# Two attention layers with products inserted between the steps: shorter insertions at fixed steps, values returned sooner

## The chip, the cores and the metric

One core of one Trainium2 chip. The time is device microseconds (us) of one execution of the whole kernel. Matrix products run on TensorE (PE), elementwise work on VectorE (DVE), exponentials and copies on ScalarE (ACT), some small work and DMA issues on GpSimd (POOL), further DMA issues on SyncE (SP). Matmuls write to PSUM, from which ACT and DVE read; everything else lies in SBUF or, between stages, in device memory.

## What is computed

Two layers, each an attention block and a Fourier mixing block, on a sequence of 2048 rows of 640 numbers, with 32 heads of 20:

```python
def _A_ref(x, wqkv, wo):
    qkv = (x @ wqkv).reshape(B, S, 3, H, Dh).transpose(2, 0, 3, 1, 4)
    q, k, v = qkv[0], qkv[1], qkv[2]
    scores = jnp.einsum("bhqd,bhkd->bhqk", q, k) * (Dh ** -0.5)
    p = _softmax(scores, axis=-1)
    o = jnp.einsum("bhqk,bhkd->bhqd", p, v)
    return o.transpose(0, 2, 1, 3).reshape(B, S, D) @ wo
def _B_ref(x, dft_seq_re, dft_seq_im, dft_hid_re, dft_hid_im):
    a = jnp.einsum("bsd,ed->bse", x, dft_hid_re)
    b = jnp.einsum("bsd,ed->bse", x, dft_hid_im)
    return jnp.einsum("ts,bse->bte", dft_seq_re, a) - jnp.einsum("ts,bse->bte", dft_seq_im, b)
x = A_x
x = x + _A_ref(_layernorm(x), A_wqkv, A_wo)
x = x + _B_ref(_layernorm(x), ...)
x = x + _A_ref(_layernorm(x), A_wqkv, A_wo)
x = x + _B_ref(_layernorm(x), ...)
```

## The kernel before

**Steps.** The attention of a layer is 512 steps, in `Attention.sweep`. A step n is a group g of four heads (eight groups), a query block qb of 512 queries (four) and a key chunk kc of 128 keys (sixteen), kc running fastest, so kc is n mod 16. `scores(n, j)`, called for j = 0 and 1, does two matmuls (L517, two heads) into one of three PSUM tiles `p`, and one exponential on ACT (L520) from there into one of seven `e` tiles. `values(n)` does the four heads' products of `e` and v (L528, eight matmul records) into the PSUM tile `acc`, of which there is one; after kc = 15 `finish` transposes it on DVE (L535), divides by the sums and stores the block (L549). Values run behind the scores: `owed = n - 1 - done` is 1 when the values of step n - 2 are due at step n.

**What is inserted.** The attention of a layer starts when one chunk of 128 columns of q and one of k are made. The rest is a generator, `Qkv.work`, that yields blocks: four chunks of q and k, the second half of v, four more chunks. For a chunk and a block of 512 tokens (tb) a product is fifteen matmuls of 128x512 (L99) into the single PSUM tile `fill`, cut by `pieces`; behind the last piece `keep` splits the product on DVE (L84, L87, and the squares at L201) and stores it (L207), and the block yields a function `after`, which makes the norms (a matmul L212 that reads the squares, a maximum on DVE at L213) and, at the end of a chunk, splits the weights of the next. The last block computes a bound on the scores, with one tiny matmul in its `after`. When the generator ends, `done()` queues the loads of the next stage's weights as tasks.

**The order by hand.** Every step of `sweep` calls `fill(n)`, which runs a waiting `after` when its step has come, or else the next block if `rest` has passed and the line `due` allows it. Before step `THIN` = 236, 80 blocks are laid down (600 matmuls); from there 16 blocks (two chunks, pieces of eight and seven) follow a straight line to step 414. If `fill` ran a block at a step from THIN on, and fewer than three values are owed, the values of that step are held back, and at a step not before `calm` two sets are done at once, unless the set to be done ends a query block. `need` forces blocks when the coming group's q and k are not made; the last chunk of q is wanted by steps 368 (tb 0), 389, 405 and 421 (tb 3).

**DVE besides.** `compare` runs up to two checks of the Fourier matrices per step on DVE (L763, L767) with loads from POOL.

Of the kernel before, what the change touches and what calls it, by code (L numbers as in the profile page):

```python
# [19 lines left out]
ND = D // 128  # L20
NT = S // 128
# [14 lines left out]
def mha_fnet_kernel(ctx, tc, x_in, wqk, wv, wo, seq, hid, nat_seq, nat_hid, out):  # L36
# [65 lines left out]
    def pieces(blocks, n):  # L102

        todo = [f for b in blocks for f in b]
        for i in range(0, len(todo), n):
            for f in todo[i:i + n]:
                f()
            yield i + n < len(todo)
# [23 lines left out]
    class Qkv:  # L132
        def __init__(s, L, src):
            s.L, s.src = L, src
            s.xn, s.xt, s.rs, s.v = {}, {}, {}, {}
            s.scr = {qk: dr.tile([D, 2, S], F32, name=f"scr{qk}_{L}") for qk in "qk"}
            s.shift = {n: dr.tile([H, 2, c], F32, name=f"shift{n}_{L}") for n, c in (("b", 512), ("m", S))}
            s.n = 1
            s.made, s.raw = set(), {}


        def load(s, k):
# [238 lines left out]
        def work(s):  # L381

            order = [ND + 1, 1, ND + 2, 2, ND + 3, 3, ND + 4, 4]
            w = {0: s.w1}

            def chunk(i):
                c = order[i]
                for tb in range(NB):
                    p = bank("fill", [128, 512], "pqk")
                    for more in pieces([s.product(p, w[i], tb, dc) for dc in range(ND)], 8):  # L390
                        if more:
                            yield True
                    sq = s.keep(p, c, tb, True, s.fill)

                    def after():
                        s.norms(bank("fill", [H, 512], "pn"), c, tb, sq)
                        s.made.add((c, tb))
                        if tb == NB - 1:
                            s.made.add(c)
                            if i + 1 < len(order):  # L400
                                w[i + 1] = s.weights(s.fill("w", [2, ND, 128], F32R, "wqk"), order[i + 1], True)
                            if i + 2 < len(order):
                                s.fetch(order[i + 2])
                    yield after

            for i in range(4):
                yield from chunk(i)
            for t in range(NT):
                p = bank("fill", [128, HD], "pv")
                for more in pieces([s.value(p, t, dc) for dc in range(ND)], 8):  # L410
                    if more:
                        yield True
                s.own(p, t, 1, True)
                yield None
            s.made.add("v")
            for i in range(4, 8):
                yield from chunk(i)

            r = s.bounds()
            ok = const.tile([128, 1], F32, name="ok", bufs=2)  # L420
            V.tensor_scalar(ok[:H], r[:H, 2:3], (GUARD / SCALE) ** 2, None, op0=OP.is_le)

            def after():
                p = bank("fill", [1, 1], "pok")
                PE.matmul(p, ok[:H], one[:H], start=True, stop=True)
                V.tensor_scalar(s.flag, p, float(H), None, op0=OP.is_equal)
            yield after
# [25 lines left out]
    class Attention:  # L453
# [98 lines left out]
        def sweep(s, shift, begin, fill):  # L552
            done = calm = 0
            for n, (g, qb, kc) in enumerate(s.steps):
                begin(n, g, qb, kc)
                last = qb == NB - 1
                if kc == (7 if last else 10 if g == LATE else 4) and not (last and g == H // 4 - 1):
                    s.qload(*((g, qb + 1) if not last else (g + 1, 0)), shift)
                if last and g + 1 < H // 4:
                    for f, j in {1: [(0, 0)], 9: [(0, 1)], 11: [(1, 0)]}.get(kc, []):  # L560
                        s.kload(g + 1, f, j)
                if qb == 0 and kc == 0 and g:
                    s.kload(g, 1, 1)
                s.scores(n, 0)
                s.scores(n, 1)

                more, owed = fill(n) and n >= 2 and n + 1 < len(s.steps), n - 1 - done
                if n < s.THIN:  # L570
                    if more and kc != 1:
                        continue
                    count = owed
                else:
                    if more and owed < 3:
                        calm = n + 6
                        continue
                    count = min(owed, 1)
                    if owed > 1 and (done + 1) % NT and n >= calm:
                        calm = n + 6  # L580
                        count = 2
                for _ in range(count):
                    s.values(done)
                    done += 1
            for n in range(done, len(s.steps)):
                s.values(n)

        def run(s, done, project, check):

            work, tasks, later = s.a.work(), s.a.vweights(1, s.a.fill, pause=[lambda: None] * 2), list(check)  # L590
            s.work, s.blocks, s.after, s.rest, s.more, s.landed = True, 0, None, 0, False, 0

            marks = ((0, 0), (44, 16), (s.THIN, 80), (414, 96), (512, 130))

            def due(n):
                for (n0, k0), (n1, k1) in zip(marks, marks[1:]):
                    if n < n1:
                        return k0 + (k1 - k0) * (n - n0) / (n1 - n0)

            def block(n):  # L600
                try:
                    f = next(work)
                    s.blocks += 1
                    s.more = f is True
                    s.after = (n + 2, f) if f and not s.more else None
                    s.rest = n + 4 if s.after else n
                except StopIteration:
                    s.work = False
                    tasks.extend(done())

            def fill(n):
                if s.after:
                    if n >= s.after[0]:
                        f, s.after = s.after[1], None
                        f()
                elif s.work and n >= s.rest and (s.more and n < s.THIN or s.blocks < due(n + 1)):
                    block(n)
                    s.rest = max(s.rest, n + 2)
                    return s.work

            def compare(n):


                if n < 8:
                    return
                for _ in range(2):
                    if not later or n < s.landed or (len(check) - len(later)) * 490 >= n * len(check):
                        break
                    task = later.pop(0)
                    if isinstance(task, tuple):  # L630
                        s.landed = n + 5
                        task = task[1]
                    task()

            def need(n, *keys):
                while not all(k in s.a.made for k in keys):
                    if s.after:
                        fill(s.after[0])
                    else:
                        block(n)  # L640

            def begin(n, g, qb, kc):


                if qb == NB - 1 and g + 1 < H // 4:
                    when, to = 0, g + 1
                    c0, c1 = to * 80 // 128, ((to + 1) * 80 - 1) // 128
                    keys = [c0, (c1, 0) if to == LATE else c1, ND + c0, ND + c1] + (["v"] if to >= 4 else [])
                else:
                    when, to, keys = 5, g, [(ND - 1, qb + 1)]  # L650
                if to != g or g == LATE and qb < NB - 1:
                    if kc == when:
                        need(n, *keys)
                        s.shift = s.a.bound(to, s.room)
                    if kc - when in (0, 3, 5):
                        next(s.shift)

                if tasks and n % 2 == 0 and n >= 16 and n % 64 < 54:
                    tasks.pop(0)()
                for f in project.early.get(n, []):  # L660
                    f()

            def between(n):
                more = fill(n)
                compare(n)
                return more

            s.sweep("b", begin, between)
            assert not s.work and not later and not tasks, (len(later), len(tasks))
# [857 lines left out]
```

## Time and profile before

| | us |
|---|---|
| median of 3 runs | 2545.14 (2545.03 to 2545.29) |
| span of the profiled execution, first to last instruction | 2543.2 |
| the median less the span (launch and end; the profiled execution has no other time recorded) | 1.9 |
| PE busy, matmuls | 2507.9 |
| ACT busy | 2136.9 |
| ACT busy in exponentials (L520) | 1938.1 |
| PE busy in values (L528), scores (L517) | 1061.5, 815.1 |
| DVE busy | 977.0 |
| POOL busy | 520.3 |

How the views are read: the page groups instructions by line, engine and tiles, with busy time and the idle time before them; a row of the timeline is start, duration, engine, line, operation, output and inputs, number of instructions merged, and in brackets the idle time before it with what released it; a row of stretches is the stretch, its length, then for each engine the busy time and the number of instructions, then the granted clock, the share of the DMA engines and GB/s. PE stands for matmuls and PEld for weight loads, which overlap them. A wait is put down to the engine and line that released it.

### The profile page before, as it was taken

The page shows a single profiled execution, that of the slowest core. Times are in us where ns is not written, and L with a number is a line of the kernel's source. Part 1 is how long each engine was busy: PE and PEld are TensorE (multiplying, and loading weights), DVE is VectorE, ACT ScalarE, POOL GpSimd, SP SyncE. Part 2 cuts the span into 40 slices and gives each one's busy share as a digit, 9 for nine tenths or more (in the row PEclk, how much of TensorE's full clock was granted, in tenths as well). Part 3 has the DMA queues.
Part 4 walks back from the last instruction along what each step waited for, and adds up shares of the span by engine and source line. Part 5 has one row for each costly group of instructions (what it writes and reads, how often), then busy time and mean ns, then how long its engine had stood idle before and what let it go on. Part 6 is the DMA issues. An engine that isn't in the chain of part 4 may idle for free. (4 is left out here: it accounts for less than half of the span.)

```text
span 2543.2 us, 43630 instructions
## 1 busy us (share of the span) xinstructions
PE 2507.9 (99%) x16350; PEld 1153.8 (45%) x16350; DVE 977.0 (38%) x2114; ACT 2136.9 (84%) x2430; POOL 520.3 (20%) x1022
## 2 busy tenths in 40 slices
PE   8999999999999999999999999999999999999998
PEld 7544444443333332239885444444433333322596
DVE  6245422244333233426763343223332323232275
ACT  6688899988999999985457888999899999999752
POOL 2012111112111121113321121111111111131133
PEclk9999999999999999999999999999999999999999
DMA  5224221222322233327553332212221212133365
GB/s 186 97 85 129 87 80 45 86 89 87 95 76 84 76 95 109 117 81 244 192 180 105 110 114 82 84 52 75 85 84 48 82 50 79 51 92 101 104 220 192
DMA packets 127024, 262.52 MB, mean 103 GB/s; under 512 B 28736, under 2 KB 53088, under 8 KB 126804
## 3 DMA queue, kind: packets, MB, share of 16 engines
q1 hardware_dynamic: 88212, 159.79, 19.2%
q0 software_dynamic: 38592, 99.85, 12.5%
q8 instruction: 132, 2.16, 0.4%
q14 instruction: 88, 0.72, 0.1%
HBM read 175.29 MB, written 84.21 MB: 102 GB/s over the span
## 5 line engine op out<-in xcount | busy, mean ns | idle before, releaser
L520 ACT ACTIVATE e<-psc 128x1024 f32<-128x1024 f32 x2048 | 1938.1, 1115 | 156.3 <-PE psc L517 119.7
L528 PE MATMUL acc<-e,v 128*32 128x512 f32 x8192 | 1061.5, 602 | 3.8 <-DVE of L535 3.3
L517 PE MATMUL psc<-stq,stk 62*128 62x512 f32 x4096 | 815.1, 463 | 3.0 <-ACT e L520 3.0
L517 PEld LDWEIGHTS psc<-stq,stk 62*128 62x128 f32 x4096 | 341.3, 184 | 835.4 <-ACT e L520 787.3
L528 PEld LDWEIGHTS acc<-e,v 128*32 128x32 f32 x8192 | 187.5, 108 | 365.8 <-issue 338.3
L549 POOL DMA_DIRECT2D o<-oh x256 | 131.9, 523 | 1002.0 <-DVE oh L544 1000.7
L99 PE MATMUL pqk<-xt,wqk 128*128 128x512 f32 x1200 | 313.8, 405 | 3.7 <-DVE wqk L84 1.5
L99 PEld LDWEIGHTS pqk<-xt,wqk 128*128 128x128 f32 x1200 | 214.7, 188 | 89.2 <-issue 37.4
L535 DVE STREAM_TRANSPOSE of<-acc 128x512 f32<-128x512 f32 x64 | 45.9, 717 | 543.0 <-PE acc L528 543.0
L84 DVE CAST hl<-pqk 128x512 fp32r<-128x512 f32 x64 | 44.2, 691 | 455.2 <-PE pqk L99 455.2
L99 PE MATMUL pv<-wv,xt 128*128 128x320 f32 x960 | 159.8, 317 | 0.0
L99 PEld LDWEIGHTS pv<-wv,xt 128*128 128x128 f32 x960 | 141.1, 188 | 25.5 <-issue 21.5
L549 POOL DMA_DIRECT2D o<-ot x256 | 128.6, 510 | 1.3 <-issue 0.4
L207 POOL DMA_DIRECT2D scrq<-hl x40 | 28.2, 706 | 388.4 <-DVE hl L87 264.2
L763 DVE TENSOR_REDUCE far<-cq 128x1 f32<-128x512 f32 (+5 forms) x169 | 98.5, 584 | 5.7
L92 PE MATMUL py<-wo,o 128*128 128x320 f32 x320 | 99.2, 310 | 1.4 <-DVE xr L945 1.4
L94 PE MATMUL py<-wo,o 128*128 128x320 f32 x320 | 98.6, 308 | 0.0
L93 PE MATMUL py<-wo,o 128*128 128x320 f32 x320 | 98.6, 308 | 0.0
L767 DVE TENSOR_TENSOR cq<-cq 128x512 f32<-128x512 f32 (+4 forms) x166 | 96.4, 580 | 2.7 <-DMA cq<-in_nat_seq_dram 2.7
L243 DVE COPY v<-pv 128x320 f32<-128x320 f32 x32 | 15.7, 491 | 204.1 <-PE pv L99 204.1
L207 POOL DMA_DIRECT2D scrk<-hl x40 | 27.9, 698 | 298.3 <-DVE hl L87 248.7
L213 DVE TENSOR_REDUCE top<-pn 32x1 f32<-32x512 f32 x80 | 53.4, 675 | 31.3 <-PE pn L212 31.3
(200 smaller groups left out, 1720.7 us busy)
## 6 DMA issues: line engine op xcount, KB each, us to landing
cq<-in_nat_seq_dram POOLq DMA_DIRECT2D x64, 512.0 KB, 5.4
scrq<-hl POOLq DMA_DIRECT2D x40, 512.0 KB, 3.2
scrk<-hl POOLq DMA_DIRECT2D x40, 512.0 KB, 3.5
stq<-scrq SPq DMA_DIRECT2D x256, 80.0 KB
stk<-scrk SPq DMA_DIRECT2D x128, 160.0 KB
o<-o SPq DMA_DIRECT2D x16, 1280.0 KB
stq<-scrq SPq DMA_DIRECT2D x256, 40.0 KB
stk<-scrk SPq DMA_DIRECT2D x128, 80.0 KB
```

What stands on the lines that cost most here:

```text
L92: PE.matmul(out_ap, ah, bh, start=start, stop=False)
L93: PE.matmul(out_ap, ah, bl, start=False, stop=False)
L94: PE.matmul(out_ap, al, bh, start=False, stop=stop)
L99: yield lambda i=i, j=j, k=k: PE.matmul(out_ap, a[i], b[j], start=dc == 0 and k == 0, stop=dc == ND - 1 and k == 2)
L207: G.dma_start(s.scr["qk"[k]][c * 128:(c + 1) * 128, :, tb * 512:(tb + 1) * 512], hl.bitcast(F32))
L213: V.tensor_reduce(s.top[:H, c // ND, c % ND, tb:tb + 1], p, op=OP.max, axis=AX.X)
L517: PE.matmul(p[:, i], s.k[g, kc // 8, j][r, kc % 8 * 128:(kc % 8 + 1) * 128], s.q[g, qb, j][r], start=True, stop=True)
L520: A.activation(e, p, AF.Exp, scale=SCALE)
L528: PE.matmul(s.acc[32 * j:32 * j + 32], s.a.v[kc][:, v0:v0 + 32], s.e[n, j // 2][:, j % 2], start=kc == 0, stop=kc == NT - 1, skip_group_ch ...
L549: G.dma_start(s.o[k, h * DH:(h + 1) * DH, qb * 512:(qb + 1) * 512], hl[k][32 * j:32 * j + DH])
L763: V.tensor_reduce(to, x, op=OP.max, axis=AX.X, apply_absolute_value=True)
L767: V.tensor_tensor(y, x, y, op=op)
```

## The change

From step 236 on, the products of q and k are inserted in pieces of five matmuls, three per product and 24 in all, at fixed steps: n mod 16 in 2, 7, 12 before step 271, and 2, 10 from there, instead of on a straight line (`rest` still applies). The norms come four steps after the last piece instead of two, and the next block not before two steps after the norms. Values held back return from n + 2 on instead of n + 6. When the generator has reached its last block (`silent`), values are no longer held back for it; it and the end of the generator follow as soon as `rest` allows.

```diff
@@ class Qkv
-            s.made, s.raw = set(), {}
+            s.made, s.raw, s.silent = set(), {}, False
@@ def work
-                    for more in pieces([s.product(p, w[i], tb, dc) for dc in range(ND)], 8):
+                    for more in pieces([s.product(p, w[i], tb, dc) for dc in range(ND)], 8 if i < 6 else 5):
...
             for i in range(4, 8):
                 yield from chunk(i)
 
+            s.silent = True
             r = s.bounds()
@@ def sweep
                     if more and owed < 3:
-                        calm = n + 6
+                        calm = n + 2
                         continue
                     count = min(owed, 1)
                     if owed > 1 and (done + 1) % NT and n >= calm:
-                        calm = n + 6
+                        calm = n + 2
                         count = 2
@@ def run
-            marks = ((0, 0), (44, 16), (s.THIN, 80), (414, 96), (512, 130))
+            marks = ((0, 0), (44, 16), (s.THIN, 80))
 
             def due(n):
                 for (n0, k0), (n1, k1) in zip(marks, marks[1:]):
                     if n < n1:
-                        return k0 + (k1 - k0) * (n - n0) / (n1 - n0)
+                        return s.blocks < k0 + (k1 - k0) * (n - n0) / (n1 - n0)
+                return s.blocks < 80 or s.blocks >= 104 or (n - 1) % NT in ((2, 7, 12) if n < 272 else (2, 10))
 
             def block(n):
...
-                    s.after = (n + 2, f) if f and not s.more else None
-                    s.rest = n + 4 if s.after else n
+                    s.after = (n + (2 if n < s.THIN else 4), f) if f and not s.more else None
+                    s.rest = s.after[0] + 2 if s.after else n
...
-                elif s.work and n >= s.rest and (s.more and n < s.THIN or s.blocks < due(n + 1)):
+                elif s.work and n >= s.rest and (s.more and n < s.THIN or due(n + 1)):
                     block(n)
                     s.rest = max(s.rest, n + 2)
-                    return s.work
+                    return s.work and not s.a.silent
```

## The prediction

> **What bounds the kernel now.** I read the page first, for the size of the parts.
>
> ```profile
> span 2543.2 us, 43630 instructions
> ...
> PE 2507.9 (99%) x16350; PEld 1153.8 (45%) x16350; DVE 977.0 (38%) x2114; ACT 2136.9 (84%) x2430; POOL 520.3 (20%) x1022
> ...
> PEclk9999999999999999999999999999999999999999
> ...
> L520 ACT ACTIVATE e<-psc 128x1024 f32<-128x1024 f32 x2048 | 1938.1, 1115 | 156.3 <-PE psc L517 119.7
> L528 PE MATMUL acc<-e,v 128*32 128x512 f32 x8192 | 1061.5, 602 | 3.8 <-DVE of L535 3.3
> L517 PE MATMUL psc<-stq,stk 62*128 62x512 f32 x4096 | 815.1, 463 | 3.0 <-ACT e L520 3.0
> ```
>
> PE looks full, but the exponentials of L520 are two per step of attention, 1024 per layer, and that line is busy for three quarters of the span. To see which of the two ends last, I looked at L520 alone in stretches. The first row below holds 472 exponentials, so 609.15 is the first of step 236 in layer 0; 1870.51 is the same place in layer 1. The next stretch of each layer is 376 exponentials, steps 236 to 423 (the count of 377 takes in one that straddles the edge), and the last is 176, steps 424 to 511.
>
> ```profile
> 87.16:609.15 521.99, 456.88 (x472) 1.00 0.28 87
> 609.15:972.56 363.41, 350.70 (x377) 1.00 0.27 83
> 972.56:1133.90 161.34, 161.34 (x177) 1.00 0.33 102
> 1347.42:1870.51 523.09, 456.81 (x472) 1.00 0.27 86
> 1870.51:2233.30 362.79, 350.66 (x377) 1.00 0.23 65
> 2233.30:2394.80 161.50, 161.50 (x177) 1.00 0.29 85
> ```
>
> In steps 424 to 511 nothing is inserted and ACT is busy all the time: 161.34 / 176 = 0.917 us for each exponential, 1.834 for a step. At that pace the 376 of the middle stretch would need 344.7 us. They took 363.4 and 362.8. So inserted work costs 18.7 us in layer 0 and 18.1 us in layer 1, and these 36.8 us are all that this change can reach: steps before 236 keep their pieces of eight and their waiting rules. For the middle stretch of layer 0 the view of L520's waits gives:
>
> ```profile
>   PE psc L517: 8.2, 30
>   PE acc L528: 4.0, 17
> ```
>
> ACT idles 12.2 us there, in 47 pieces. The rest is restart: exponentials overlap in a train and do not behind a gap. A train of 13 takes 12.04 us, so (12.04 - 1.02) / 12 = 0.918 each, against 1.03 for one alone; each of the 47 gaps costs 0.11 more, 5.2 us. 12.2 + 5.2 = 17.4 of the 18.7.
>
> ```profile
> 612.92 12.04 ACT L520 ACTIVATE e<-psc 128x1024 f32<-128x1024 f32 x13 [0.20 <-PE acc L528]
> ```
>
> **The price of one piece before.** The timeline of steps 258 and 259, a piece of eight with its step's values left out, then a step with one set of values:
>
> ```profile
> 650.62 0.91 PE L517 MATMUL psc<-stq,stk 62*128 62x512 f32 x4
> 651.02 0.19 PEld L517 LDWEIGHTS psc<-stq,stk 62*128 62x128 f32 x2 [0.22 <-ACT e L520]
> ...
> 651.45 2.10 PE L99 MATMUL pqk<-xt,wqk 128*128 128x512 f32 x8
> 653.49 0.30 PEld L517 LDWEIGHTS psc<-stq,stk 62*128 62x128 f32 x4 [0.35 <-issue]
> 653.49 0.73 PE L517 MATMUL psc<-stq,stk 62*128 62x512 f32 x4
> 654.09 1.03 ACT L520 ACTIVATE e<-psc 128x1024 f32<-128x1024 f32 x1 [0.37 <-PE psc L517]
> 654.15 1.06 PE L528 MATMUL acc<-e,v 128*32 128x512 f32 x8
> 655.14 0.30 PEld L517 LDWEIGHTS psc<-stq,stk 62*128 62x128 f32 x4 [0.84 <-ACT e L520]
> 655.14 0.73 PE L517 MATMUL psc<-stq,stk 62*128 62x512 f32 x4
> 655.31 1.03 ACT L520 ACTIVATE e<-psc 128x1024 f32<-128x1024 f32 x1 [0.20 <-PE acc L528]
> ```
>
> Scores hold PE for 0.66 (653.49 to 654.15) and one set of values for 0.99, so a plain step needs 1.65 of PE and 1.83 of ACT: PE gains 0.18 of lead per step until it has to wait for a score buffer, as at 651.02. The piece of eight holds PE 2.04. Behind it ACT waits twice: 0.37 for scores, and 0.20 for the values that free the next of seven e buffers. With two restarts the piece costs 0.37 + 0.20 + 0.22 = 0.79. The rows below hold the two other parts. A piece of seven holds PE 674.57 - 672.76 = 1.81, so one matmul is 0.23, and its price is 0.79 - 0.23 = 0.56. Some steps after a piece the withheld values come back, two sets in one step (663.30), 1.85 of PE, and ACT waits 0.25, with the restart 0.36:
>
> ```profile
> 663.30 1.92 PE L528 MATMUL acc<-e,v 128*32 128x512 f32 x16
> ...
> 665.15 0.73 PE L517 MATMUL psc<-stq,stk 62*128 62x512 f32 x4
> 665.75 1.02 ACT L520 ACTIVATE e<-psc 128x1024 f32<-128x1024 f32 x1 [0.25 <-PE psc L517]
> ...
> 672.76 1.88 PE L99 MATMUL pqk<-xt,wqk 128*128 128x512 f32 x7
> 674.57 0.30 PEld L517 LDWEIGHTS psc<-stq,stk 62*128 62x128 f32 x4 [0.35 <-issue]
> ```
>
> There are eight products per layer left at step 236 (two chunks by four token blocks), each 15 matmuls, so 8 x (0.79 + 0.56 + 2 x 0.36) = 16.6. To that comes one norms product that waits for DVE's squares, at step 404:
>
> ```profile
> 931.21 0.73 PE L517 MATMUL psc<-stq,stk 62*128 62x512 f32 x4
> ...
> 933.83 0.68 DVE L201 TENSOR_TENSOR sq<-hl 128x512 bf16<-128x512 f32 x1
> ...
> 934.56 0.38 PE L212 MATMUL pn<-sq,ind 128*32 128x512 bf16 x1 [0.96 <-DVE sq L201]
> ...
> 935.91 1.94 ACT L520 ACTIVATE e<-psc 128x1024 f32<-128x1024 f32 x2 [0.94 <-PE acc L528]
> ...
> 967.12 23.94 ACT L520 ACTIVATE e<-psc 128x1024 f32<-128x1024 f32 x26 [0.17 <-PE psc L517]
> ```
>
> That is 0.94 + 0.11 = 1.05. The last row is the values withheld at step 414 for a block that inserts no matmul of size, returned at 420: 0.17 + 0.11 = 0.28. Sum 16.6 + 1.05 + 0.28 = 17.9 against 18.1 and 18.7 found. The prices account for the stretch.
>
> **The change part by part.** *Pieces of five instead of eight and seven.* Each product becomes three pieces, 24 per layer instead of 16. The second exponential behind a piece is tied to PE: it starts 655.31 - 653.49 = 1.82 after the scores that follow the piece, so its delay falls by what the piece is shorter: 0.79 - 3 x 0.23 = 0.10 for five. PE then holds 1.35 in place of 0.99.
>
> By the Trainium skill (TensorE: Matmul & The Clock Gate, section Back-to-back issue gap) a 512-column matmul takes 518 cycles, 0.216 us, behind another; three fewer would then save 0.65 and not 0.69, the price would be 0.14, and the estimate of the total 2 us higher. The rows above have 0.23, and I keep that.
>
> *Values back at n + 2 instead of n + 6.* This is the disputed part: PE has had no time to rebuild its lead. Call T the start of the scores in step n + 1. The second exponential of that step starts at T + 1.82, and in a train the first of step n + 3 would start three later, at T + 1.82 + 3 x 0.918 = T + 4.57. PE starts step n + 2 at T + 1.65, spends 0.66 + 1.85 on scores and two sets of values, starts step n + 3 at T + 4.16, and 0.60 after that (653.49 to 654.09) the exponential can start: T + 4.76. It is late by 0.19. So the early return is not dearer than the old one; ACT was already held up 0.10 by the piece and PE works at 1.65 meanwhile. Bounds: 0.19 by this walk, 0.36 by the row of the old returns. I take 0.25, nearer to the walk, because it uses PE times from rows of just such steps.
>
> *The next piece.* From step 274 pieces stand 8 apart (step mod 16 is 2 or 10), from 236 to 268 five, six or eleven. A slot at 252 is in the list but not usable: the third piece at 247 puts its norms at 251 and rest at 253. So the pieces stand at 236, 242, 247, 258, 263, 268, 274, 282 and so on to 410: 24. PE's work over 8 steps with one piece is 8 x 0.66 + 6 x 0.99 + 1.85 + 1.35 = 14.4, ACT's 14.7. It just fits. At a distance of five: from the scores of step n + 3 at U (exponential at U + 0.60) PE reaches the scores behind the next piece at U + 2 x 1.65 + 0.66 + 1.35 = U + 5.31, and the tied exponential at U + 7.13, against U + 0.60 + 7 x 0.918 = U + 7.03. Again 0.10.
>
> *Norms product at n + 4.* The squares at 404 were ready at 934.51, 3.30 after the piece's end (931.21). In the new order PE reaches the norms product after 1.65 + 2.51 + 1.65 + 0.66 = 6.5. The 1.05 goes. If it returned at the three third pieces that stand right behind the block's end (290, 338, 386), 3.2 would be added.
>
> *Silent end.* No values are withheld for the bounds block any more: 0.28 goes. The loads for the next stage start four steps later, at 422 instead of 418. I cost that at nothing: ninety steps of attention still cover them. If that cover were gone it would be those four steps, 4 x 1.83 = 7.3 in each layer. DMA issues keep their number: eight stores of hl, the same o and weight loads, on the same queues.
>
> Sum per layer: 24 x (0.10 + 0.25) = 8.4, with ends 24 x (0.10 + 0.19) = 7.0 and 24 x (0.10 + 0.36) + 3.2 = 14.2. Layer 0's surplus of 0.6 over layer 1 stays. Saved: 18.1 - 8.4 = 9.7 per layer, 19.4 in two; the ends are 22 and 8. The profiled span is 2543.2, 1.9 below the median of 2545.1, which adds what lies around it and does not change. 2545.1 - 19.4 = 2525.7, so 2526, between 2523 and 2537.
>
> **The rivals.** *PE is the real bound*, as its 99% say. Then only PE's work counts: three fives hold it 4.05 against 2.04 + 1.81, +0.20 per product, less 0.13 for one more doubled return (2 x 0.99 - 1.85): 16 x 0.07 = +1.1, 2546. Against it: 1.65 per step against 1.83, and PE waiting on ACT at 651.02.
>
> *The early return meets PE with no lead at all.* Then three steps cost what PE needs, 2.01 + 1.65 + 2.51 = 6.17 against 5.50: 0.67 x 24 = 16.1 per layer, 2.0 saved each, 2541. For it: the order of events above leaves no spare step. Against: the walk.
>
> *Slower: the norms product waits for DVE every time.* PE runs in order, so scores queue behind it and ACT behind them. The block's end puts a chain on DVE, and the checks put pairs there:
>
> ```profile
> 622.00 0.72 DVE L535 STREAM_TRANSPOSE of<-acc 128x512 f32<-128x512 f32 x1 [9.40 <-PE acc L528]
> ...
> 625.19 0.69 DVE L545 TENSOR_TENSOR ot<-ot,oh 128x512 f32<-128x512 f32 x1
> ...
> 626.07 0.67 DVE L767 TENSOR_TENSOR cq<-cq 128x512 f32<-128x512 f32 x1
> ...
> 626.78 0.69 DVE L763 TENSOR_REDUCE far<-cq 128x1 f32<-128x512 f32 x1
> ```
>
> A further chain (3.88) and a pair (1.36) ahead of the squares make 3.3 + 5.2 = 8.5, 2.0 later than PE arrives; with a restart 2.1 x 8 = 16.8 per layer, 25.2 with the 8.4, 7.1 more than now: 2559. It decides from a cost of 9.7 / 8 = 1.2 at every product. Against: DVE is 38% busy, and of the eight norms products of layer 0 one waited, at half the distance:
>
> ```profile
>   DVE sq L201: 1.0, 1
> ```
>
> *Returns cost nothing*: 24 x 0.10 = 2.4, 15.7 saved per layer, 2514. The walk speaks against it.
>
> *The slots don't hold*: if one more slot were lost the last norms would fall at 422, behind the demand of step 421, and PE would wait about 1 us in each layer: 2528.
>
> **How the numbers follow.** Forecast 0.78, slots 0.04, free returns 0.05: together 0.87 faster by over 0.2% (5 us, about what a measurement of this kernel can tell from no change). PE bound 0.03 and no lead 0.04 are within it: 0.07. Slower: 0.06, the DVE wait and what I have not seen. The range runs from 2519, where half of the returns is hidden, to 2539, a little beyond the dear end of the sum; it leaves out the rivals at 2514, 2541, 2546 and 2559 and a little of the forecast's own tails, 0.2 in all.
>
> **What would show it.** In the timeline from step 236: ACT trains broken by two short gaps per piece, about 0 to 0.1 us at the next step (released by L528's acc) and 0.1 to 0.25 at the step behind the doubled values (released by psc), no longer 0.37 and more; no L212 with an idle time released by DVE; the stretch of 376 exponentials at 353 us per layer; the stretches before step 236 unchanged at 522 and 523. It is wrong if gaps of 0.3 and more stand behind the returns, if PE waits for DVE at the norms, or if the last stretch grows by what the middle one lost.

## The result

2524.36 us (2523.62 to 2524.84) against 2545.22 for the kernel before, 20.9 less: a ratio of 0.9918, interval 0.9904 to 0.9932. The forecast was 2526, 19.4 less.

The stretches of the exponentials' line, which is L521 now since the change adds a line above it (values are L529), show where it went. Columns: the stretch, its length, ACT busy in that line and the number, granted clock, DMA share, GB/s. The first three are steps 0 to 235, 236 to 423 and 424 to 511 of layer 0, the others the same of layer 1 up to 423.

```profile
span 2522.9 us, 43616 instructions
...
87.57:609.52 521.95, 456.85 (x472) 1.00 0.28 87
609.52:961.81 352.29, 349.44 (x378) 1.00 0.28 86
961.81:1122.10 160.29, 160.29 (x177) 1.00 0.34 102
1337.49:1860.62 523.13, 456.82 (x473) 1.00 0.27 86
1860.62:2212.90 352.28, 349.43 (x377) 1.00 0.23 68
```

The first and last stretches are what they were: 521.99 and 523.09 before for the first; the 160.29 and the 161.34 of before are cut at different points inside the last exponential, and from end to end the 176 take 161.33 in both kernels. The middle fell from 363.41 to 352.29 and from 362.79 to 352.28: 11.1 + 10.5 = 21.6. The span fell by 20.3, so 1.3 went elsewhere: 0.4 ahead of the first exponential (87.58 against 87.17), 0.6 between the layers (214.0 against 213.4 from the last exponential's end to the next one's start), and 0.3 lies in where the stretches are cut. Of the 18.7 and 18.1 us that inserted work cost per layer, 7.6 are left (352.3 - 344.7). The stretches run from start to start; from the end of one exponential to the end of another it is 352.5, which is nearer to the 7.75 that the expectations below use.

What L521 waited for in the middle stretch of layer 0 (us, times):

```profile
  PE acc L529: 0.2, 1
```

And the norms product L212 in the same stretch:

```profile
  issue: 2.9, 8
```

Before, these were 8.2 and 4.0 us of idle ACT in 47 places, and one norms product waited 1.0 for DVE. Now one idle place of 0.2 is listed, and no wait for DVE. But 7.6 us are lost all the same. An exponential that comes 0.1 or 0.2 late still begins before or shortly after the last one ends, so it loses its overlap with it and leaves little idle time. The stretch has 2.85 of ACT's idle time (352.29 less 349.44), in pieces too short for the list; the other 4.7 is lost overlap, which counts as busy. Neither number alone shows the loss; the length of the stretch does. The timeline of one period, steps 258 to 261:

```profile
650.73 1.43 PE L99 MATMUL pqk<-xt,wqk 128*128 128x512 f32 x5
652.08 0.73 PE L518 MATMUL psc<-stq,stk 62*128 62x512 f32 x4
...
653.74 0.73 PE L518 MATMUL psc<-stq,stk 62*128 62x512 f32 x4
...
654.40 1.92 PE L529 MATMUL acc<-e,v 128*32 128x512 f32 x16
...
656.26 0.73 PE L518 MATMUL psc<-stq,stk 62*128 62x512 f32 x4
```

Five matmuls hold PE for 1.35 (650.73 to 652.08), as worked out from the pieces of eight and seven. With T = 652.08 the next scores start at T + 1.66 and the scores behind the doubled values at T + 4.18; the walk had T + 1.65 and T + 4.16. ACT over the same time is one unbroken row:

```profile
647.26 19.02 ACT L521 ACTIVATE e<-psc 128x1024 f32<-128x1024 f32 x20
```

In a train 20 exponentials would take 19 x 0.917 + 1.03 = 18.45. Of the 0.57 more, 0.47 are three delays around the pieces of 258 and 263 (0.10, 0.21 and 0.16 by the ends of the exponentials), without a gap that would split the row. Over the stretch it is 7.6 / 24 = 0.32 per piece. Measured from the end of each exponential to the end of the next, it is 0.10 to 0.16 at the second one behind a piece and 0.20 to 0.24 behind the doubled values, and next to nothing elsewhere; only the very first piece costs 0.30, at step 237.

### The profile page after: what moved, and what is told of

The parts are those of the page before. It is cut to its first block, busy times and chain, and to the rows that moved or that the text cites. A ratio compares the mean times of both kernels' runs of the same rounds, so it can differ in the third digit from the quotient of the medians.

```text
span 2522.9 us, 43616 instructions
## 1 busy us (share of the span) xinstructions
PE 2492.9 (99%) x16350; PEld 1152.7 (46%) x16350; DVE 976.4 (39%) x2114; ACT 2134.2 (85%) x2430; POOL 520.5 (21%) x1022
## 5 line engine op out<-in xcount | busy, mean ns | idle before, releaser
L521 ACT ACTIVATE e<-psc 128x1024 f32<-128x1024 f32 x2048 | 1935.9, 1128 | 137.1 <-PE psc L518 103.7
L529 PE MATMUL acc<-e,v 128*32 128x512 f32 x8192 | 1058.6, 602 | 1.9 <-DVE of L536 1.8
L518 PE MATMUL psc<-stq,stk 62*128 62x512 f32 x4096 | 799.3, 458 | 1.3 <-ACT e L521 1.3
L529 PEld LDWEIGHTS acc<-e,v 128*32 128x32 f32 x8192 | 188.9, 108 | 370.0 <-issue 344.7
L84 DVE CAST hl<-pqk 128x512 fp32r<-128x512 f32 x64 | 44.2, 690 | 432.2 <-PE pqk L99 432.2
L99 PEld LDWEIGHTS pv<-wv,xt 128*128 128x128 f32 x960 | 141.2, 188 | 25.5 <-issue 21.6
```

The costliest lines, as they stand in the source:

```text
L99: yield lambda i=i, j=j, k=k: PE.matmul(out_ap, a[i], b[j], start=dc == 0 and k == 0, stop=dc == ND - 1 and k == 2)
L518: PE.matmul(p[:, i], s.k[g, kc // 8, j][r, kc % 8 * 128:(kc % 8 + 1) * 128], s.q[g, qb, j][r], start=True, stop=True)
L521: A.activation(e, p, AF.Exp, scale=SCALE)
L529: PE.matmul(s.acc[32 * j:32 * j + 32], s.a.v[kc][:, v0:v0 + 32], s.e[n, j // 2][:, j % 2], start=kc == 0, stop=kc == NT - 1, skip_group_ch ...
```

## The experiments

The theory: ACT bounds these steps; what is lost is what PE's order makes an exponential late, 0.10 behind a piece of five (tied to PE through the values that free its e buffer) and 0.20 behind the return at n + 2 (PE's excess of a double step, less the lead it then has). The rivals: the early return alone is the gain; the fixed steps alone are; PE's total work is the bound. In the following the stretch is always that of the 376 exponentials of steps 236 to 423, layer 0 then layer 1, and the loss its length less 344.7.

**One part at a time.** The kernel before with the early return alone, the same edit in both places (`e1_return`):

```diff
-                        calm = n + 6
+                        calm = n + 2
```

> The kernel before with one edit: values return from n + 2 instead of n + 6; pieces of eight and seven on the straight line stay. Theory (ACT is held up by what PE does between two scores, and only a short piece shortens that): a return at n + 2 costs about 0.2 behind a piece of eight, but behind a piece of seven it falls on the step of the norms product and costs about 0.4, against 0.30 to 0.38 before; under 1 us per layer saved, 2543 to 2545, stretch of 376 exponentials 362 to 363.5. Rival (the early return is the gain): most of the 21 us is here, 2531 or less.

2546.64 us, ratio to the kernel before 1.0006 (0.9997 to 1.0015): no gain. The stretches:

```profile
609.00:971.78 362.78, 350.30 (x377) 1.00 0.27 84
1869.76:2232.20 362.44, 350.36 (x378) 1.00 0.22 66
```

0.6 and 0.4 shorter than before, as the theory has it, and too little to be seen in the time. The time itself was forecast at 2543 to 2545 and came out 1.6 above: in the profiled execution 2.3 more lie behind the last exponential of layer 1 (150.7 against 148.4), a stage that the edit does not touch; why was not tried. The early return is not the gain by itself.

The changed kernel with pieces of eight and seven again, at its fixed steps (`e3_eight`):

```diff
-    ... pieces([s.product(p, w[i], tb, dc) for dc in range(ND)], 8 if i < 6 else 5):
+    ... pieces([s.product(p, w[i], tb, dc) for dc in range(ND)], 8):
-                return s.blocks < 80 or s.blocks >= 104 or ...
+                return s.blocks < 80 or s.blocks >= 96 or ...
```

> The changed kernel with pieces of eight and seven again (16 instead of 24), at the same fixed steps, values back at n + 2. Theory: a piece costs 0.79 or 0.56 and a return 0.2 to 0.4, about 14.4 lost per layer instead of 7.75, 2538. Rival (the fixed steps are the gain): 2526 or less, since fewer pieces are inserted.

2538.84 (ratio 0.9974, 0.9964 to 0.9984).

```profile
609.04:967.67 358.63, 349.25 (x378) 1.00 0.31 92
1867.47:2226.53 359.06, 349.66 (x378) 1.00 0.26 74
```

Losses 13.9 and 14.4, forecast 14.4. Fixed steps, later norms, early return and silent end together give 6.6 us; cutting the products into fives gives the other 14.5 (2538.84 to 2524.36). By the ends of the exponentials a piece of eight costs about 0.79 and one of seven about 0.56 here, and the return behind either 0.20 to 0.23, as behind fives.

**When the values return.** `calm` set to n + 1, n + 3 or n + 4 in both places of the changed kernel (`e8_next`, `e9_three`, `e2_late`):

```diff
-                        calm = n + 2
+                        calm = n + 1    # e8_next; n + 3 in e9_three, n + 4 in e2_late
```

> The changed kernel with values back from n + 1. Theory: with two sets in step n + 1 PE starts the scores of n + 2 at T + 2.51, their exponential at T + 3.11 instead of T + 1.82 + 0.92 = T + 2.74: 0.37 late instead of 0.2, about 11.8 lost per layer instead of 7.75, 2532.5. Rival (the sooner the better): 2524 or less.

> The changed kernel with values back from n + 3. Theory: by then PE has caught up with ACT and waits for a score buffer ahead of the double step, 0.3 late instead of 0.2, about 10.5 lost per layer, 2530; n + 2 is the cheapest of n + 1 to n + 4. Rival (later is better, PE has more lead): under 2524.

> The changed kernel with one edit: values return from n + 4 (n + 6 cannot be had with pieces five steps apart). Theory: two steps later PE waits for score buffers again, the return costs 0.3 and more as in the old order, and the lead is not back at the next piece; about 12.5 lost per layer instead of 7.75, 2534. Rival (the pieces are all of the gain, the return is free): 2524 to 2526.

The stretches of e8_next:

```profile
609.08:965.55 356.47, 349.39 (x378) 1.00 0.28 84
1864.15:2220.37 356.22, 349.40 (x378) 1.00 0.23 67
```

Of e9_three:

```profile
609.23:964.59 355.36, 349.70 (x378) 1.00 0.27 85
1862.84:2218.22 355.38, 349.79 (x377) 1.00 0.23 67
```

And of e2_late:

```profile
609.05:966.94 357.89, 350.73 (x377) 1.00 0.27 84
1864.98:2222.89 357.91, 350.71 (x378) 1.00 0.23 67
```

| values back from | time, us | ratio to before (interval) | loss per layer |
|---|---|---|---|
| n + 1 | 2532.05 | 0.9949 (0.9936 to 0.9963) | 11.8, 11.5 |
| n + 2 | 2524.36 | 0.9918 (0.9904 to 0.9932) | 7.6, 7.6 |
| n + 3 | 2529.58 | 0.9938 (0.9925 to 0.9952) | 10.7, 10.7 |
| n + 4 | 2534.79 | 0.9960 (0.9946 to 0.9974) | 13.2, 13.2 |

All three were forecast within 1 us. Neither sooner nor later is better. The timeline of e8_next, steps 259 and 260, has an idle time that n + 2 avoids:

```profile
652.39 0.73 PE L518 MATMUL psc<-stq,stk 62*128 62x512 f32 x4
...
654.91 0.73 PE L518 MATMUL psc<-stq,stk 62*128 62x512 f32 x4
655.51 4.69 ACT L521 ACTIVATE e<-psc 128x1024 f32<-128x1024 f32 x5 [0.27 <-PE psc L518]
```

Scores at T + 2.52, exponential at T + 3.12 with 0.27 of idle time and 0.11 of restart, 0.38: the 0.37 of the walk. With eights and sevens the return hardly matters (`e1_return`), with fives there are 10.4 us between n + 2 and n + 4, and at n + 4 the fives save only 10.6. The two edits belong together.

**How short.** Pieces of 4, 4, 4 and 3, 32 per layer, five to six steps apart (`e7_four`):

```diff
-    ... 8 if i < 6 else 5):
+    ... 8 if i < 6 else 4):
-    ... s.blocks >= 104 or (n - 1) % NT in ((2, 7, 12) if n < 272 else (2, 10))
+    ... s.blocks >= 112 or (n - 1) % NT in (2, 7, 12)
-    s.rest = s.after[0] + 2 if s.after else n
+    s.rest = s.after[0] + (2 if n < s.THIN else 1) if s.after else n
```

> The changed kernel with pieces of 4, 4, 4 and 3 instead of three fives, 32 per layer, at n mod 16 = 2, 7, 12 throughout, next piece allowed one step after the norms. Theory: behind a piece of four ACT is not held up any more, so the return takes the whole blow, 0.31 each: 32 x 0.31 = 9.8 lost per layer instead of 7.75, 2528.5. Rival (the shorter the better): 32 x 0.2 = 6.4, 2522 or less.

2529.77 (ratio 0.9939, 0.9925 to 0.9952). The stretches:

```profile
609.11:963.03 353.92, 348.08 (x378) 1.00 0.28 87
1861.48:2215.44 353.96, 348.07 (x377) 1.00 0.24 69
```

What L521 waited for in the first:

```profile
  PE psc L518: 5.3, 27
```

9.2 and 9.3 lost, forecast 9.8, and a time 1.3 above the forecast; the listed waits for values are gone, and the 27 listed returns wait 0.20 for scores (5.3 / 27), 0.31 with the restart. Shorter is not better: what the piece spares, the return takes, and there are 32 returns for 24. The Trainium skill (Perfetto Trace Analysis, section Matmul Optimizations) asks for matmuls back to back in batches, because the engine scales its power with its use; it names no size of a batch. The granted clock is 1.00 in the stretches with eights, with fives and with fours, so in these runs the clock does not choose between them: eights are worse because they hold ACT up longer, fours because there are more returns.

**Norms two steps after the piece** (`e4_norms`), pieces where they were:

```diff
-    s.after = (n + (2 if n < s.THIN else 4), f) if f and not s.more else None
-    s.rest = s.after[0] + 2 if s.after else n
+    s.after = (n + 2, f) if f and not s.more else None
+    s.rest = s.after[0] + (2 if n < s.THIN else 4) if s.after else n
```

> The changed kernel with the norms two steps after the last piece, the next piece where it was. Theory: the norms product then shares the step with the doubled values, 0.2 dearer at each of eight: 2527. If PE also waits for DVE's squares at the three last pieces that stand behind the end of a block (290, 338, 386), 1.05 each: 2533. Rival (the four steps matter nowhere): 2524.

2535.62 (ratio 0.9960, 0.9947 to 0.9974), above the forecast of 2527 and of 2533 with the waits. The stretches:

```profile
609.12:967.19 358.07, 349.90 (x378) 1.00 0.27 84
1865.42:2223.53 358.11, 349.91 (x378) 1.00 0.23 66
```

What L212 waited for in layer 0's stretch, besides its own issue:

```profile
  DVE sq L201: 4.2, 3
```

What L521 waited for there:

```profile
  PE acc L529: 4.3, 4
  PE psc L518: 2.0, 8
```

And the timeline of steps 291 and 292:

```profile
713.50 0.69 DVE L546 TENSOR_TENSOR ot<-ot,oh 128x512 f32<-128x512 f32 x1
...
714.11 0.68 DVE L84 CAST hl<-pqk 128x512 fp32r<-128x512 f32 x1
...
715.43 0.68 DVE L201 TENSOR_TENSOR sq<-hl 128x512 bf16<-128x512 f32 x1
716.17 0.38 PE L212 MATMUL pn<-sq,ind 128*32 128x512 bf16 x1 [1.40 <-DVE sq L201]
...
717.51 1.02 ACT L521 ACTIVATE e<-psc 128x1024 f32<-128x1024 f32 x1 [1.37 <-PE acc L529]
```

The three waits are at 292, 340 and 388, two steps behind the pieces at 290, 338 and 386 that follow a block's end: the product's split (L84) queues on DVE behind the block's chain (L546 its last). Each costs 1.37 + 0.11 = 1.48, not 1.05: at 404 in the old kernel the piece was longer by 0.46, so DVE's chain was that much nearer to its end when the product was made, and the squares were ready 3.30 after the piece and not 3.73 as here. With the norms in the doubled step, 0.16 more at each of eight returns (0.36 for 0.20 by the ends of the exponentials), that is 3 x 1.48 + 8 x 0.16 = 5.7 per layer of the 5.8 found (loss 13.4). So four steps instead of two are worth 11.3 us once the pieces are at fixed steps behind the block's end; in the old order only one product in eight met the wait.

**Which steps** (`e5_slots`):

```diff
-    ... (n - 1) % NT in ((2, 7, 12) if n < 272 else (2, 10))
+    ... (n - 1) % NT in ((2, 7, 12) if n < 272 else (6, 14))
```

> The changed kernel with the pieces from step 271 on at n mod 16 = 6 and 14 instead of 2 and 10. Theory (only length, spacing and return count): no change, 7.7 lost per layer, 2524. Rival (a piece at 2 stands where the first values of a block would wait for DVE's transposition of the last block, and hides that wait): 8 to 9 pieces per layer lose about 0.2 more, 2528.

2527.20 (ratio 0.9928, 0.9915 to 0.9942), between the two forecasts.

```profile
608.93:963.44 354.51, 349.49 (x378) 1.00 0.27 84
1861.83:2214.95 353.12, 349.56 (x377) 1.00 0.22 65
```

Layer 1 loses 0.8 more than the changed kernel: returns at the first step of a block cost 0.23 to 0.25 instead of 0.20, and two of them (behind 320 and 384) 0.35. That is a small effect of the place. Layer 0 loses another 1.4, at five returns 32 steps apart (281, 313, 345, 377, 409), one of which reads:

```profile
693.39 0.73 PE L518 MATMUL psc<-stq,stk 62*128 62x512 f32 x4
694.26 3.77 ACT L521 ACTIVATE e<-psc 128x1024 f32<-128x1024 f32 x4 [0.37 <-PE psc L518]
```

The exponential starts 0.87 after its scores instead of 0.60. It was free to start: ACT's record of the wait ends at 693.94, and the exponential starts 0.32 later, where 0.05 is usual. This does not belong to these slots. In layer 0 of every run the first exponential of a step 25 above a multiple of 32 starts 0.32 to 0.34 behind the end of its wait where it has to wait: at 25, 57, 89, 153, 185 and 217 in all runs, at 281 and 409 in the kernel before, at 249 in `e8_next`. That is one place in 64 exponentials. In layer 1 only `e3_eight` shows it, at 22 above a multiple of 32 (22, 86, 118, 150, 214). What ACT does there stays open; in the changed kernel no return falls on these steps. That a piece at step 2 hides the wait for the transposition is not shown.

**Silent** (`e11_silent`, one profiled run): `return s.work` instead of `return s.work and not s.a.silent`.

> The changed kernel without silent: values are held back again for the block that computes the bounds. Theory: one more return near step 418, 0.2 to 0.4 per layer, seen as one more gap of ACT behind step 416 in the trace, 2525. Rival: nothing is seen there.

2524.94, a single time and just above the range of the changed kernel; the stretches:

```profile
609.20:962.09 352.89, 349.73 (x378) 1.00 0.27 84
1860.65:2213.61 352.96, 349.75 (x377) 1.00 0.23 66
```

The timeline at step 420:

```profile
954.84 2.86 ACT L521 ACTIVATE e<-psc 128x1024 f32<-128x1024 f32 x3 [0.27 <-PE psc L518]
```

0.6 and 0.7 more by these stretches, of which 0.2 lies in where they are cut (the first exponential of step 424 starts less early inside the one before); from end to end it is 0.4 and 0.5. In layer 0 the row above is nearly all of it, 0.27 + 0.11 behind the doubled values of step 419.

**The return in halves** (`e10_halves`). If the excess of one double step is what a return costs, spreading it over two steps should take it away. The second set is done for query columns 0 to 255 in step n + 2 and for the rest in n + 3:

```diff
-        def values(s, n):
+        def values(s, n, half=None):
+            c = slice(None) if half is None else slice(256 * half, 256 * half + 256)
...
-                PE.matmul(s.acc[32 * j:32 * j + 32], ..., s.e[n, j // 2][:, j % 2],
+                PE.matmul(s.acc[32 * j:32 * j + 32, c], ..., s.e[n, j // 2][:, j % 2, c],
...
-            if kc == NT - 1:
+            if kc == NT - 1 and half != 0:
...
                         calm = n + 2
-                        count = 2
+                        s.values(done)
+                        done += 1
+                        s.values(done, 0)
+                        rest = done
+                        continue
+                    if rest is not None:
+                        s.values(rest, 1)
+                        done, rest = done + 1, None
```

> The changed kernel, but the second of the two returned sets is done in halves of 256 query columns: the first half in step n + 2, the second ahead of the values of step n + 3. Theory: PE's excess per step is then 0.25 instead of 0.68, and the exponentials behind the return start on time (PE reaches the scores of n + 4 at T + 5.81, exponential T + 6.41; train T + 6.41): about 4.3 lost per layer instead of 7.75, 2517.5. Rival (PE's work is the bound, and a set in halves is no less of it): 2524 to 2526.

2520.83 (2518.82 to 2521.57), ratio to the kernel before 0.9900 (0.9883 to 0.9916). The stretches:

```profile
609.21:958.35 349.14, 348.08 (x377) 1.00 0.28 86
1860.49:2209.61 349.12, 348.04 (x377) 1.00 0.24 68
```

The timeline of steps 259 to 262 (values are L530 here):

```profile
651.49 0.73 PE L518 MATMUL psc<-stq,stk 62*128 62x512 f32 x4
...
653.81 1.50 PE L530 MATMUL acc<-e,v 128*32 128x512 f32 x16
...
655.24 0.73 PE L518 MATMUL psc<-stq,stk 62*128 62x512 f32 x4
...
655.90 1.50 PE L530 MATMUL acc<-e,v 128*32 128x256 f32 x16
...
657.33 0.73 PE L518 MATMUL psc<-stq,stk 62*128 62x512 f32 x4
```

The loss falls from 7.6 to 4.4 per layer, as forecast (4.3): PE reaches the scores behind the return at T + 5.84, the walk had T + 5.81. PE has no less to do, so the rival that its work is the bound falls. PE is listed as busy for all of the stretch in both kernels, 352.29 of 352.29 before the halves and 349.12 of 349.14 with them: its listed busy time shrank with the stretch, and being listed as full does not make it the bound. Not all is gain: behind four of the pieces that stand five or six steps after another the tied exponential is now 0.28 to 0.31 late, for 0.12 to 0.16 with whole sets. Of the 6.3 us saved in the stretches 3.5 show in the median. The four times lie 2.7 apart, and the profiled execution is the slowest (2521.57); there the rest is ahead of the attention of layer 1, which the edit does not touch: from the end of the last exponential of layer 0 to the first of layer 1 it took 217.4 (1120.0 to 1337.4) against 214.0 in the changed kernel. The list of waits has there (waiting line, releaser; us, times, longest):

```profile
ACT hl L204 <- issue: 5.9, 3, 2.3
ACT hl L204 <- DMA d_x<-xd: 2.0, 1, 2.0
```

That of the changed kernel has the first too, but shorter, and not the second:

```profile
ACT hl L204 <- issue: 4.6, 2, 2.3
```

Whether these waits are the 3.4 was not tried. The intervals of the two versions overlap, so that this one is the faster is shown in the two stretches and not beyond doubt in the total. Two deeper tests were not run: eight e buffers, which would cut the tie behind the piece, and a return at n + 6 with fives.

## Why the prediction was right

**What bounds.** Right. The first and the last stretches stood still, the middle moved by all of the gain, and the return in halves and the curve over n + 1 to n + 4 move the time with PE's order at equal work. The middle saved 21.6 (21.3 from end to end), about 2 more than the 19.4 of the forecast; the 1.0 lost ahead of the attention and between the layers, which the prediction put at nothing, brought the total nearer to it, and that was luck.

**Price of a piece of five.** 0.10 by the tie; 0.10 to 0.16 found. The figure of the Trainium skill (TensorE: Matmul & The Clock Gate, section Back-to-back issue gap) that the prediction weighed, 0.216 per matmul, is given there for a matmul taken by itself; for a stream of weight loads and matmuls the section gives about 0.131. Estimated from these, five would hold PE for 2.04 - 0.65 = 1.39 or 2.04 - 0.39 = 1.65; the trace has 1.35, as 0.23 per matmul gives.

**Price of a return at n + 2.** This is the term that was mis-sized. The walk gave 0.19 and the old returns 0.36, and I took 0.25; 0.20 to 0.24 were found, 0.20 in most. The old returns do not price the new one: they are dearer, by the theory because PE had caught up with ACT and waited for a buffer in the same step. With n + 3 a return costs 0.29 to 0.32 and with n + 4 0.29 to 0.39. The row of 0.36 was also one of the dear ones, most of the old returns cost about 0.30. Sum 24 x (0.10 + 0.25) = 8.4 against 7.6.

**Layer 0's surplus of 0.6.** Assumed to stay; it went. Both layers now take 352.3. Two exponentials made nearly all of it, the first of step 409 (0.57 late against 0.30 in layer 1, one of the late starts of `e5_slots`) and the second of step 339 (0.35 against 0.10).

**Norms at n + 4.** That the 1.05 goes was right, and so was the place where it would come back (e4_norms). Its price was 1.48 and not 1.05; the dear end of the sum was too low by 1.3 per layer for that.

**Silent.** 0.28 forecast, 0.4 to 0.5 measured from end to end, on a part that I had priced by one gap. The 7.3 per layer, the price if nothing covered the later loads, is not there: behind the last exponential 0.6 was added in layer 0 (up to the first exponential of layer 1) and 0.1 saved in layer 1 (up to the end).

**The rivals.** PE as the bound and a return with no lead: both fall with the stretches of 352.3, and 0.67 per piece would be 16.1 where 7.6 were found. Norms that wait for DVE every time: not in the changed kernel; at half the distance three of eight do. The slots held, with 252 left out and the last piece at 410 as worked out. Returns at no cost: not here; in halves they cost 0.03 to 0.06 each.

**What would show it.** I looked for short gaps of 0.1 to 0.25 in the list of idle times. There is one of 0.2 in a whole layer. The delays are there, but a delay of 0.2 is 0.11 of lost overlap and 0.09 of idle time, too short for the list. The forecast for the stretch, 353, was the better test.

## What to carry to other kernels

When one engine feeds another through a few buffers, price an insertion by how late it makes the next consumer, from the times in the trace; pieces just short enough to be swallowed by the lead, and the deferred work put back where the consumer is already held up, beat both longer pieces and more of them. Walk three or four steps by hand with measured durations before choosing the step of the return: one step either way cost 5 to 8 us here. Measure a bound engine by the length of a stretch with a known count, cut at the ends of its instructions, and not by its idle time.

## What the runs showed of the hardware

Exponentials of 128x1024 overlap by about 0.11 when they follow one another (0.917 apart, 1.03 alone), and short delays eat that overlap before much idle time shows: 7.6 us were lost in a stretch with 2.85 us of idle time, 0.2 of it listed. The Trainium skill (ScalarE: Activation LUTs, section What ACT_TABLE_LOAD costs) gives an overlap of about 93 ns for activations back to back, near to what is seen here. Matmuls of 128x256 with four heads side by side take half the time of those of 128x512: a set and a half with the switch held PE 1.43 (653.81 to 655.24) against 0.99 for one set (654.15 to 655.14 in the kernel before) and 1.86 for two whole sets (654.40 to 656.26 in the changed kernel). At one place in 64 exponentials of layer 0 an exponential that had to wait started 0.32 to 0.34 behind the end of its wait instead of 0.05, in all twelve traces; in layer 1 one run alone (`e3_eight`) shows it. It is not explained.
